# Retention plus phase-MLP kernel on one core: half of the fourth unit's output copy behind the fifth unit's masking, the sixth unit's scores ahead of the fifth's inner product

## The chip, the cores and the metric

One core of a Trainium2 chip runs the kernel. The metric is the device time of one execution in microseconds (us); lower is better. The kernel before was run three times: 164.02, 164.14 and 164.96 us, median 164.14 us.

Engine names below: PE multiplies matrices (PEld is its weight load), DVE is the vector engine, ACT the activation engine, POOL the general-purpose engine, SP the engine that only issues transfers. PE writes into PSUM banks; DVE and ACT read them from there.

## The reference: what is computed

Inputs are q, k and v of shape (4 batches, 8 heads, 768 positions, 64 columns) and four weight matrices. The first part is a recurrent retention per batch and head, the second a small phase network on its output:

```python
for t in range(S):
    state = gamma * state + outer(k[t], v[t])
    y[t] = scale * (q[t] @ state)
x = y with the heads side by side            # (4, 768, 512)
theta = x @ w_theta
zr, zi = x * cos(theta), x * sin(theta)
u = x + w_tok_r @ zr + w_tok_i @ zi          # mixes the 768 positions
out = u + maximum(u @ w_ch, 0)
```

## The kernel before: tiles, stages and what sets the order

The recurrence is computed in blocks. A *unit* is 256 positions of four heads of one batch, so there are 4 x 3 x 2 = 24 units, numbered from 0 in the code. Unit 3 is the fourth unit, unit 4 the fifth, unit 5 the sixth. Two successive units hold the same positions and the two halves of the heads. A unit passes through these steps:

- `ck`, `cq` or `cqs`, `cv`: k, q and v, as loaded, become bfloat16 (line 350 for v, tile `vb`).
- `Tk`, `Tq` (line 358): PE transposes k and q into one PSUM tile `kq_ps`; `E` copies it to `kqT` in SBUF, on ACT (line 138) or DVE (line 140).
- `A` (line 392): PE computes the *scores*, 16 small matmuls of `kqT` with itself, into the PSUM tile `at_ps`. There is one buffer of it. `m` (line 401, DVE) multiplies the scores by the causal mask into `at`.
- `I` (line 457): the *inner product* of q with the state carried from before (`sbd`), four matmuls; `Y` (line 469): the masked scores times v, 16 small matmuls added to the same PSUM tile; `ST` (line 419): the state's increment, 16 small matmuls into another part of that tile. The tile is `r_ps`, in two banks R0 and R1, one buffer each, so a unit's `I` waits until the unit before it has been read out of both.
- `S0`, `S1` (lines 437 and 441, DVE) add the increment to the state `s`; `SB` casts it into `sbd` for the next unit of the same heads, one half on each of two engines.
- `XB` (a copy, line 138 or 140) or `XA` (a multiplication, line 487): the *output copy*, which takes the unit's result from R0 (c = 0) and R1 (c = 1) into `xT`. This is in two halves, one for each bank.
- `Tx`, `Ex`: `xT` is transposed (line 501) and copied to `x_sb`; `Hh` (line 518) multiplies it with w_theta; `CN` (line 525, ACT) takes sine and cosine; `z` (line 532) multiplies. `Tw` and `Ew` (lines 540 and 140) transpose the token-mixing weights, `M` (line 563) sums over positions, `u`, `Tu`, `O`, `f` and `SO` form and store the output.

The order of all this is written out by hand: `ORDER` (lines 23 to 87) is a string of tokens, one for each step, and the kernel calls them in that order. A token's last letter names the engine (`v` DVE, `a` ACT, `p` POOL, `s` SP). No scheduler reorders: each engine executes its own instructions in the order in which the tokens issue them, and waits where an operand or a buffer is not ready. `XB.3.1.v` is thus the copy of half 1 of unit 3 on DVE, `m.4` the masking of unit 4, `E.5.v` the copy of unit 5's transposed k and q on DVE, `A.5` unit 5's scores, and `I.4` unit 4's inner product.

Of the kernel before, what the change touches and what calls it, by code (L numbers as in the profile page):

```python
# [28 lines left out]
Z.11 cqs.3.p Tq.3 Lv.3.s Tx.0 Tk.3 Z.3 ck.4.p Lv.4.s Lk.5.s Lq.5.s Lv.5.s Lq.6.s Lk.6.s Lv.6.s Lq.7.s E.3.a  # L29
SB.2.0.v I.2 Y.2 XB.2.1.a Ex.0.a cv.3.v cq.4.p Tk.4 Lq.8.s A.3 ST.3 Lk.7.s S0.3.v SB.3.0.a S1.3 Lv.7.s  # L30
Lk.8.s Tx.1 Tq.4 SB.3.1.p cv.4.p m.3 Pw.1.0 XB.2.0.a Ex.1.a I.3 Lv.8.s E.4.a cq.5.a Y.3 Pw.0.0 ST.4 Hh.0
ck.5.a S0.4.v XB.3.0.v XB.3.1.v cv.5.v CN.0.1 A.4 CN.0.0 Tq.5 Hh.1 Tk.5 SB.4.0.p SB.4.1.a Pw.0.1 Hh.2 m.4
E.5.v I.4 Y.4 ST.5 ck.6.a Tk.6 Tx.2 cq.6.a CN.1.1 CN.1.0 XA.4.1 A.5 XA.4.0 m.5 Lq.9.s Ex.2.v S0.5.v z.0.p
Tq.6 E.6.a CN.2.0 cv.6.p Hh.3 SB.5.0.v Tx.3 Tw.1.0 z.1.v SB.5.1.a Ew.1.0.v Ex.3.a CN.2.1 A.6 I.5 Y.5 ST.6
XA.5.0 z.2.v Tw.0.0 CN.3.0 Tx.4 CN.3.1 Ew.0.0.v S0.6.v XA.5.1 Ex.4.v Hh.4 CN.4.0 CN.4.1 Tw.0.1 M.0.1 Pw.1.1
z.3.v M.0.0 Tw.0.2 Pw.1.2 Ew.0.2.a SB.6.1.a Hh.5 z.4.p SB.6.0.p Lk.9.a M.0.3 ck.7.p cqs.7.p M.0.2 CN.5.1
# [770 lines left out]
```

## Time and profile before

| | before |
|---|---|
| runs, us | 164.02, 164.14, 164.96 |
| the profiled execution, us | 164.45 |
| its span, us | 162.7 |
| PE busy, us | 152.1 |
| DVE busy, us | 128.4 |
| ACT busy, us | 82.8 |
| POOL busy, us | 80.7 |
| granted clock of PE, share of full speed | 0.996 |

The span runs from the first to the last instruction of the profiled execution; the 1.7 us between it and that execution's time lie around the kernel. All positions in time below are us from the span's start. In a row of the timeline, several instructions of the same kind that follow each other are one row with their count, and an instruction's duration includes a part that overlaps the next one, so the distance between two starts is shorter than the duration. A remark in brackets says how long the engine had been idle before the row, and who ended that wait.

### The profile page before, as it was taken

The numbers are of one execution on the slowest core, as the hardware profiler recorded it, in microseconds if no ns is written. First come the engines' busy times: TensorE is split into PE (matmuls) and PEld (weight loads), VectorE is DVE, ScalarE is ACT, GpSimd is POOL, SyncE is SP. The second block draws the span as 40 slices with busy tenths as digits, with TensorE's granted clock in tenths as the row PEclk, the third lists the DMA queues.
The fourth block names the chain that finished last, engine by engine and source line by source line (L and its number), as shares of the span: only waits on it lengthen the run. The fifth ranks groups of instructions, "written<-read, shape, count | busy, mean of one in ns | idle before, by whom it ended". The sixth has DMA issues, their size and how long they took to land.

```text
span 162.7 us, 5046 instructions
## 1 busy us (share of the span) xinstructions
PE 152.1 (93%) x2043; PEld 90.8 (56%) x2072; DVE 128.4 (79%) x254; ACT 82.8 (51%) x151; POOL 80.7 (50%) x115
## 2 busy tenths in 40 slices
PE   5997979999999999999999999999999999999991
PEld 1354656656666555754454656544555446788650
DVE  5489687977993896994879796967988898796782
ACT  4967698994658336664443526761755506100010
POOL 7788089169206732550227499966468601540000
PEclk9999999999999999999999999999999999999998
DMA  4999999999999998969999998899999416533845
GB/s 123 319 309 236 298 318 244 265 229 216 202 208 195 308 236 190 276 153 266 317 318 204 124 296 137 214 185 266 233 275 142 82 28 181 160 118 102 225 170 219
DMA packets 62919, 34.93 MB, mean 215 GB/s; under 512 B 26416, under 2 KB 59952, under 8 KB 62896
## 3 DMA queue, kind: packets, MB, share of 16 engines
q1 hardware_dynamic: 51680, 23.73, 66.0%
q10 hardware_dynamic: 8528, 7.47, 15.4%
q0 software_dynamic: 2688, 3.41, 12.4%
q8 instruction: 16, 0.26, 0.7%
q14 instruction: 7, 0.06, 0.1%
HBM read 25.69 MB, written 6.29 MB: 197 GB/s over the span
## 4 chain that ended last, share of the span: by engine, by line
PE 85%; DVE 4%; ACT 4%; issue 2%; DMA 2%; POOL 0%; DVEq 0%; SPq 0%; POOLq 0%
PE y_ps L563 27%; PE th_ps L518 12%; PE o_ps L593 12%; PE zz L313 5%; PE r_ps L469 4%; PE kq_ps L358 4%; PE xw L681 3%; PE at_ps L392 3%; PE xwv L681 3%; PE w_ps L540 3%; PE r_ps L457 3%; PE vv L681 3%; PE x_ps L501 2%; DMA out_dram<-ot 2%; PE r_ps L419 2%
## 5 line engine op out<-in xcount | busy, mean ns | idle before, releaser
L563 PE MATMUL y_ps<-z,wti 128*128 128x512 bf16 x105 | 39.8, 379 | 1.2 <-issue 1.1
L563 PE MATMUL y_ps<-z,wtr 128*128 128x512 bf16 x100 | 37.9, 379 | 0.1
L401 DVE TENSOR_TENSOR at<-at_ps,mask 128x1024 bf16<-128x1024 f32 x24 | 29.2, 1217 | 0.1
L350 POOL TENSOR_TENSOR vb<-vf,vsc 128x512 bf16<-128x512 f32 x18 | 18.8, 1046 | 20.2 <-DMA vf<-in_v_dram 13.3
L518 PE MATMUL th_ps<-wth,xT 128*128 128x512 bf16 x88 | 24.2, 379 | 0.6
L593 PE MATMUL o_ps<-wch,uT 128*128 128x512 bf16 x85 | 22.2, 379 | 0.6 <-DMA out_dram<-ot 0.2
L525 ACT ACTIVATE cs<-th_ps,halfpi 128x512 bf16<-128x512 f32 x24 | 16.5, 686 | 10.1 <-DVE z L532 4.0
L532 POOL TENSOR_TENSOR z<-cs,x_sb 128x1024 bf16<-128x1024 bf16 x8 | 17.0, 2124 | 8.5 <-DVE z L532 4.7
L525 ACT ACTIVATE cs<-th_ps,zerob 128x512 bf16<-128x512 f32 x24 | 16.4, 685 | 8.2 <-PE th_ps L518 8.1
L138 ACT COPY kqT<-kq_ps 128x1024 bf16<-128x1024 bf16 x12 | 12.1, 1012 | 11.9 <-PE kq_ps L358 11.9
L140 POOL CAST sbd<-s 64x256 bf16<-64x256 f32 (+1 forms) x17 | 8.9, 525 | 18.3 <-DVE s L437 16.8
L599 DVE SCALAR_TENSOR_TENSOR ot<-o_ps,u 128x512 f32<-128x512 f32 x23 | 15.6, 687 | 2.7 <-PE o_ps L593 2.7
L570 DVE TENSOR_TENSOR u<-y_ps,x_sb 128x512 bf16<-128x512 f32 x18 | 12.4, 687 | 6.3 <-PE y_ps L563 6.1
L563 PEld LDWEIGHTS <-wtr 128*128 128x128 bf16 x108 | 10.5, 97 | 9.7
L563 PEld LDWEIGHTS <-wti 128*128 128x128 bf16 x108 | 10.5, 98 | 8.8 <-DVE wti L140 0.2
L518 PEld LDWEIGHTS <-xT 128*128 128x128 bf16 x96 | 8.8, 98 | 8.3
L138 ACT CAST sbd<-s 64x256 bf16<-64x256 f32 (+1 forms) x24 | 8.9, 372 | 7.8 <-DVE s L437 6.0
L593 PEld LDWEIGHTS <-uT 128*128 128x128 bf16 x92 | 8.3, 98 | 7.8 <-DMA uT<-u 0.2
L313 PE MATMUL zz<-zero 128*128 128x512 bf16 x27 | 10.1, 511 | 2.0 <-DVE part L233 1.9
L358 PE MATMUL kq_ps<-ident,kqb 128*128 128x128 bf16 x120 | 11.2, 220 | 0.8 <-ACT kqb L138 0.7
L138 ACT CAST kqb<-kqf 128x512 bf16<-128x512 f32 x17 | 10.3, 620 | 2.4 <-DMA kqf<-in_k_dram 2.3
L138 ACT CAST xT<-r_ps 128x256 bf16<-128x256 f32 x19 | 6.7, 371 | 9.3 <-PE r_ps L419 8.4
(127 smaller groups left out, 281.7 us busy)
## 6 DMA issues: line engine op xcount, KB each, us to landing
vf<-in_v_dram SPq DMA_DIRECT2D x20, 256.0 KB, 5.4
kqf<-in_k_dram SPq DMA_DIRECT2D x19, 256.0 KB, 4.6
kqf<-in_q_dram SPq DMA_DIRECT2D x17, 256.0 KB, 4.5
out_dram<-ot ACTq DMA_DIRECT2D x12, 256.0 KB, 3.1
out_dram<-ot SPq DMA_DIRECT2D x11, 256.0 KB, 2.8
kqf<-in_q_dram ACTq DMA_DIRECT2D x7, 256.0 KB, 5.0
kqf<-in_k_dram ACTq DMA_DIRECT2D x5, 256.0 KB, 5.5
vf<-in_v_dram ACTq DMA_DIRECT2D x4, 256.0 KB, 4.7
```

The source lines that it names most:

```text
L138: nc.scalar.copy(dst, src)
L313: nc.tensor.matmul(t, K["zero"][:, :P], K["zero"], start=True, stop=True)
L350: engines[e].tensor_mul(in_blocks(vb), by_token(raw["vf", n]), _bcast_last(K["vsc"][:, i, :, h * HU:(h + 1) * HU], D))
L358: nc.tensor.transpose(st["kq_ps", n][:, 4 * w + x, :], st["kqb", n][:, w, x * P:(x + 1) * P], K["ident"])
L401: nc.vector.tensor_mul(at.rearrange("p g j a t -> p (g j) (a t)"), st["at_ps", n].rearrange("p g j a t -> p (g j) (a t)"), _bcast_mid(K["m ...
L518: nc.tensor.matmul(th_ps, st["xT", C][:, j, :], K["wth"][:, j, :], start=(j == 0), stop=(j == 3))
L525: nc.scalar.activation(st["cs", C][:, w, :], st["th_ps", C], AF.Sin, bias=K["zerob" if w else "halfpi"], scale=1.0)
L532: engines[e].tensor_mul(st["z", b][:, c], st["cs", C], _bcast_mid(x_of(C), 2))
L563: nc.tensor.matmul(st["y", t], K["wT"][r][:, s0, t0 * P:(t0 + 1) * P], st["z", b][:, s0, r, :], start=(done == 0 and r == 0), stop=(done = ...
L593: nc.tensor.matmul(o_ps, st["uT", t][:, j, :], K["wch"][:, j, :], start=(j == 0), stop=(j == nD - 1))
L599: nc.vector.scalar_tensor_tensor(st["ot", t], st["o", t], 0.0, st["u", t], ALU.max, ALU.add)
L681: nc.tensor.matmul(o, a, m_, start=(phase == 0 and n == 0 and k != 1), stop=n == nT - 1, skip_group_check=True)
```

## The change

Two tokens change places in the string:

```diff
-ck.5.a S0.4.v XB.3.0.v XB.3.1.v cv.5.v CN.0.1 A.4 CN.0.0 Tq.5 Hh.1 Tk.5 SB.4.0.p SB.4.1.a Pw.0.1 Hh.2 m.4
-E.5.v I.4 Y.4 ST.5 ck.6.a Tk.6 Tx.2 cq.6.a CN.1.1 CN.1.0 XA.4.1 A.5 XA.4.0 m.5 Lq.9.s Ex.2.v S0.5.v z.0.p
+ck.5.a S0.4.v XB.3.0.v cv.5.v CN.0.1 A.4 CN.0.0 Tq.5 Hh.1 Tk.5 SB.4.0.p SB.4.1.a Pw.0.1 Hh.2 m.4 XB.3.1.v
+E.5.v A.5 I.4 Y.4 ST.5 ck.6.a Tk.6 Tx.2 cq.6.a CN.1.1 CN.1.0 XA.4.1 XA.4.0 m.5 Lq.9.s Ex.2.v S0.5.v z.0.p
```

On DVE, one copy moves past two instructions. These are DVE's rows from unit 4's state update on; the first `L140 CAST xT<-r_ps` is `XB.3.0`, the second `XB.3.1`, `L350` is `cv.5`, `L401` is `m.4`, `L140 COPY kqT` is `E.5`, and `L487` is unit 4's output copy.

```order
 L437 TENSOR_TENSOR s_444<-r_ps,s_444 128x128
-L140 CAST xT<-r_ps 128x256 x2
-L350 TENSOR_TENSOR vb<-vf,vsc 128x512
-L401 TENSOR_TENSOR at<-at_ps,mask 128x1024
+L140 CAST xT<-r_ps 128x256
+L350 TENSOR_TENSOR vb<-vf,vsc 128x512
+L401 TENSOR_TENSOR at<-at_ps,mask 128x1024
+L140 CAST xT<-r_ps 128x256
 L140 COPY kqT<-kq_ps 128x1024
 L487 TENSOR_TENSOR xT<-r_ps,qx 128x256 x2
```

The second copy now stands between `m.4` and `E.5`. The rows that follow are in the same order as before: `m.5` stays behind unit 4's two output multiplications.

On PE, the 16 matmuls and 16 weight loads of `A.5` move up. This is PE before, where the last matmuls of `Hh.2` (line 518) are followed by `I.4` (line 457):

```order
L518 MATMUL th_ps<-wth,xT 128x512
L518 LDWEIGHTS xT
L518 MATMUL th_ps<-wth,xT 128x512
L457 LDWEIGHTS sbd_96 [waits Activation_49,Pool_49]
L457 MATMUL r_ps<-kqT,sbd_96 128x128 [waits PE_49]
```

And this is the same place now, with `A.5` (line 392) behind `Hh.2`:

```order
L518 MATMUL th_ps<-wth,xT 128x512
L518 LDWEIGHTS xT
L518 MATMUL th_ps<-wth,xT 128x512
L392 LDWEIGHTS kqT [waits DVE_49]
L392 MATMUL at_ps<-kqT 64x128 [waits PE_49]
```

`I.4` comes behind `A.5`, then `Y.4`, `ST.5`, `Tk.6` and `Tx.2` as before, and then `Tq.6` directly, where `A.5` used to stand between `Tx.2` and `Tq.6`. The first weight load of `A.5` now holds a wait on DVE, for `E.5`. Nothing changes on ACT, POOL and SP, and no instruction is added or removed.

## The prediction

> **What bounds the kernel now.** I read the page first, then busy time by stage, then the timeline of PE, DVE and ACT around the change.
>
> ```profile
> span 162.7 us, 5046 instructions
> PE 152.1 (93%) x2043; PEld 90.8 (56%) x2072; DVE 128.4 (79%) x254; ACT 82.8 (51%) x151; POOL 80.7 (50%) x115
> PE 85%; DVE 4%; ACT 4%; issue 2%; DMA 2%; POOL 0%; DVEq 0%; SPq 0%; POOLq 0%
> ```
>
> The third row is the chain of work that ended last, by engine: PE holds 85% of it. By stage (columns: the stretch, its length, busy us of PE, PEld, DVE, ACT and POOL, the granted clock, the DMA share, GB/s):
>
> ```profile
> 20.00:24.00 4.00, 3.05 (x67) 1.98 (x66) 3.20 (x8) 3.94 (x8) 3.55 (x6) 1.00 1.14 315
> 24.00:28.00 4.00, 3.95 (x78) 2.64 (x77) 2.94 (x5) 3.40 (x7) 3.49 (x3) 1.00 1.16 256
> 28.00:32.00 4.00, 3.70 (x76) 2.50 (x77) 3.75 (x9) 3.93 (x7) 1.11 (x2) 1.00 1.15 262
> 40.00:60.00 20.00, 19.42 (x322) 12.33 (x326) 16.30 (x33) 11.49 (x20) 8.52 (x9) 1.00 1.18 236
> ```
>
> PE stands idle for about 1 us at 20 to 24, before the change takes hold; from 24 on it works 3.95 of 4, 3.70 of 4, 19.42 of 20. So whatever PE loses at the place of the change has little idle time behind it to be made up in, and whatever it could gain is bounded by the idle time that stands there now. PE at this place, unit by unit (start, duration, line, what, count):
>
> ```profile
> 22.08 1.04 PE L518 MATMUL th_ps<-wth,xT 128*128 128x512 bf16 x3
> 23.05 0.42 PE L392 MATMUL at_ps<-kqT 64*64 64x128 bf16 x16
> 24.50 0.39 PE L358 MATMUL kq_ps<-ident,kqb 128*128 128x128 bf16 x4
> 24.73 1.03 PE L518 MATMUL th_ps<-wth,xT 128*128 128x512 bf16 x4
> 25.59 0.40 PE L457 MATMUL r_ps<-kqT,sbd 128*128 128x128 bf16 x4
> 25.91 0.42 PE L469 MATMUL r_ps<-at,vb 64*64 64x128 bf16 x16
> 26.16 0.29 PE L419 MATMUL r_ps<-vb,kqb 64*64 64x64 bf16 x16
> 26.39 0.40 PE L358 MATMUL kq_ps<-ident,kqb 128*128 128x128 bf16 x4
> 26.62 0.39 PE L501 MATMUL x_ps<-ident,xT 128*128 128x128 bf16 x4
> 26.94 0.42 PE L392 MATMUL at_ps<-kqT 64*64 64x128 bf16 x16
> 27.29 0.40 PE L358 MATMUL kq_ps<-ident,kqb 128*128 128x128 bf16 x4
> 28.79 0.38 PE L501 MATMUL x_ps<-ident,xT 128*128 128x128 bf16 x4 [0.24 <-ACT kqT L138]
> 29.45 0.42 PE L392 MATMUL at_ps<-kqT 64*64 64x128 bf16 x16
> 29.81 0.41 PE L457 MATMUL r_ps<-kqT,sbd 128*128 128x128 bf16 x4
> 30.15 0.42 PE L469 MATMUL r_ps<-at,vb 64*64 64x128 bf16 x16
> ```
>
> These are A.4 at 23.05, Tk.5 at 24.50, Hh.2 at 24.73, I.4 at 25.59, Y.4, ST.5, Tk.6, Tx.2, A.5 at 26.94, Tq.6 at 27.29, Tx.3 at 28.79, and A.6, I.5, Y.5. Neither I.4 nor A.5 nor Y.4 waited: the only wait is 0.24 before Tx.3, for the copy E.6 on ACT. DVE in the same stretch:
>
> ```profile
> 22.23 0.29 DVE L437 TENSOR_TENSOR s<-r_ps,s 128x128 f32<-128x128 f32 x1 [0.67 <-PE r_ps L419]
> 22.43 0.75 DVE L140 CAST xT<-r_ps 128x256 bf16<-128x256 f32 x2
> 23.10 0.68 DVE L350 TENSOR_TENSOR vb<-vf,vsc 128x512 bf16<-128x512 f32 x1
> 23.69 1.22 DVE L401 TENSOR_TENSOR at<-at_ps,mask 128x1024 bf16<-128x1024 f32 x1
> 24.93 0.69 DVE L140 COPY kqT<-kq_ps 128x1024 bf16<-128x1024 bf16 x1
> 26.55 0.76 DVE L487 TENSOR_TENSOR xT<-r_ps,qx 128x256 bf16<-128x256 f32 x2 [0.93 <-PE r_ps L419]
> 27.42 1.23 DVE L401 TENSOR_TENSOR at<-at_ps,mask 128x1024 bf16<-128x1024 f32 x1
> 28.56 0.42 DVE L140 COPY x_sb<-x_ps 128x512 bf16<-128x512 bf16 x1
> 28.89 0.28 DVE L437 TENSOR_TENSOR s<-r_ps,s 128x128 f32<-128x128 f32 x1
> 30.02 0.54 DVE L140 COPY wti<-w_ps 128x768 bf16<-128x768 bf16 x1
> 30.77 0.42 DVE L487 TENSOR_TENSOR xT<-r_ps,qx 128x256 bf16<-128x256 f32 x1 [0.21 <-PE r_ps L419]
> ```
>
> S0.4, then XB.3.0 and XB.3.1 (one row, x2), cv.5, m.4, E.5, an idle 0.93, XA.4.1 and XA.4.0, m.5 at 27.42, Ex.2, S0.5, Ew.1.0, XA.5.0.
>
> **The copy XB.3.1, moved behind m.4.** The pair and its follower lie 23.10 - 22.43 = 0.67 apart, so one copy holds DVE for 0.335. Without it cv.5 starts at 22.77 and leaves DVE free at 22.77 + 0.59 (its distance to m.4) = 23.36. But m.4 also needs A.4, which ends at 23.05 + 0.42 = 23.47; m.5 started 0.06 after A.5 ended (26.94 + 0.42 = 27.36, then 27.42), so m.4 starts at 23.53, 0.16 earlier than now. Nobody waits for it sooner: Y.4, its reader, did not wait. XB.3.1 follows at 23.53 + 1.14 (the distance of m.5 to Ex.2) = 24.67 and ends at about 25.09, before I.4 needs the bank R1 that it empties. E.5 starts at 24.67 + 0.335 = 25.00. Tk.5 has ended by 24.50 + 0.39 = 24.89, so DVE itself is what E.5 waits for, and it is 0.07 late: ends 25.69 instead of 25.62. The readers of XB.3.1's own result, Hh.3 and Tx.3, come after 27.5.
>
> **A.5, moved ahead of I.4.** Its first weight load now needs E.5. What such a hand-off takes is shown by unit 0:
>
> ```profile
> 8.57 0.69 DVE L140 COPY kqT<-kq_ps 128x1024 bf16<-128x1024 bf16 x1 [1.35 <-PE kq_ps L358]
> 9.31 0.42 PE L392 MATMUL at_ps<-kqT 64*64 64x128 bf16 x16
> ```
>
> The copy ended at 9.26 and the scores started at 9.31, 0.05 later. A.5 therefore starts at 25.69 + 0.05 = 25.74. With E.5 in time it would start about 0.97 behind Hh.2 (as A.4 behind Hh.0, 22.08 to 23.05), at 25.70; the wait itself is worth about 0.04, and it is Hh.2 that hides the rest of E.5. Without that cover the price would be the whole 0.69 of the copy. As to the cost of going from large to small matmuls: Hh.2 to I.4 is 0.86, Hh.0 to A.4 is 0.97, so 0.11 goes with the switch to 64*64. [...]
>
> Behind A.5, by distances between starts: I.4 0.36 later (29.45 to 29.81) at 26.10; Y.4 0.34 later (29.81 to 30.15) at 26.44; ST.5 0.25 later at 26.69; Tk.6 0.23 later at 26.92; Tx.2 0.23 later at 27.15; Tq.6 0.23 later (as Tx.2 behind Tk.6) at 27.38. Before, Tq.6 started at 27.29. PE's own loss up to here is 0.09.
>
> **What follows from it.** ACT in this stretch:
>
> ```profile
> 27.73 1.01 ACT L138 COPY kqT<-kq_ps 128x1024 bf16<-128x1024 bf16 x1 [0.55 <-PE kq_ps L358]
> 28.64 0.69 ACT L525 ACTIVATE cs<-th_ps,halfpi 128x512 bf16<-128x512 f32 x1
> 29.36 0.40 ACT L138 CAST sbd<-s 64x256 bf16<-64x256 f32 x1
> ```
>
> E.6 waited 0.55 for Tq.6, so it moves with Tq.6 by 0.09, and so do Tx.3, which waits for E.6, and A.6. The larger delay is on DVE. ST.5 moved from 26.16 to 26.69, by 0.53, because A.5 now stands ahead of it; XA.4.1, which waited for ST.5, moves to 27.08. m.5 cannot use the scores being ready at 26.16, since it stands behind XA.4 in DVE's order: it starts 0.67 after XA.4.1, at 27.75, which is 0.33 later than now (the other 0.2 was spent waiting for A.5, or lay between XA.4 and m.5). Ex.2 follows at 28.89, S0.5 at 28.89 + 0.33 = 29.22, ending 29.50. Its reader on ACT, half of SB.5, started at 29.36 because ACT was busy until 28.64 + 0.69 = 29.33; S0.5 had ended at 29.17. Now ACT is free at 29.42 and S0.5 is done at 29.50: with the 0.05 of a hand-off it starts at 29.55, 0.19 later, and ends at 29.95. I.5 needs it. PE is ready for I.5 at 29.81 + 0.09 = 29.90; 0.05 after the cast is 30.00. So I.5 and all behind it on PE are 0.19 late. Y.5 at 30.34 finds m.5 finished (27.75 + 1.23 = 28.98). XA.5.0 waited for ST.6 with 0.21 of idle DVE; it moves by 0.19 to 30.96, while DVE, 0.33 late, finishes Ew.1.0 at 30.35 + 0.54 = 30.89 and does not add to that.
>
> Sum: 0.04 for the wait at A.5, 0.05 for the rearranged switches, 0.10 for the state cast that now ends last: 0.19 us, carried to the end by a PE that has hardly any idle time left. Against the profiled execution, 164.45 + 0.19 = 164.64; that execution was 0.31 above the median of the runs, so against the median 164.14 + 0.19 = 164.3 us.
>
> **Bounds of the unknown terms.** No row shows A.5 directly behind Hh.2, or I.4 behind A.5 here. From below: if A.5 took I.4's slot at 25.59, Tq.6 would start at 27.23, a gain of 0.06. From above: the whole 0.53 by which ST.5 moves passes on to PE. I take 0.19, near the middle, because the two waits for E.5 and for the state cast are both read from rows beside them.
>
> **The rivals.**
>
> *No loss at all* (164.1): E.5's 0.07 disappears under Hh.2 and the 0.33 of DVE under the casts, as ACT's own occupancy hid S0.5 by 0.16 until now. For it: every single term is below 0.1. Against it: the terms all have the same sign.
>
> *The whole delay reaches PE* (164.14 + 0.53 = 164.7): it happens if DVE's lateness meets a PE that waits for DVE's weight copies between 30 and 36. Against it, DVE has idle time in this row:
>
> ```profile
> 36.21 1.02 DVE L140 COPY wti<-w_ps 128x768 bf16<-128x768 bf16 x2 [0.88 <-PE w_ps L540]
> ```
>
> *Somewhat faster* (163.8): the moved order makes the 0.24 wait before Tx.3 disappear and A.5 takes I.4's slot: 0.24 + 0.06 = 0.30. For it: it is the only idle time that PE has here. Against it: Tx.3 waits for E.6 and E.6 for Tq.6, which gets no earlier than by that 0.06.
>
> *Slower by over 1%* (165.8): the lateness of the masking accumulates. Each of the units 5 to 9 has the same loop, ST to XA to m to S0 to SB to I; if PE waited in each for its state cast by the 0.33 that m.5 is late, five units would give 1.65. It decides from the point where unit 6's cast, too, ends later than PE is ready for I.6. Against it: the waits don't add when the same lateness is met again, and the 0.88 of idle DVE at 36.21 ends it.
>
> *Faster by over 1%*: this would need 1.64, and from 24 on no row at this place has PE waiting for more than 0.24.
>
> **How the numbers follow.** The forecast (late by 0.1 to 0.35) has a chance of 0.55, no loss 0.23, the whole delay 0.10, somewhat faster 0.07, slower by over 1% 0.03, faster by over 1% 0.02. About 1% is what a measurement of this kernel can tell from no change: its three runs span 0.6%. The range takes the bounds of the sum, 164.08 and 164.67, widened on either side by the 0.31 by which one execution stood off the median: 163.7 to 165.0. Within 1%, that is 162.5 to 165.8, lie all cases but the last two: 0.95.
>
> **What would show it.** In the changed kernel's timeline the scores of unit 5 should follow Hh.2 at about 25.74, with a short wait for kqT of DVE; XB.3.1 alone at about 24.67 and E.5 at 25.00; Tq.6 near 27.38; XA.4.1 near 27.08 after more than the present 0.93 of idle DVE; m.5 near 27.75 without a wait; the state cast on ACT near 29.55 and I.5 near 30.00. The prediction is wrong if Tq.6 starts before 27.29, if I.5 starts as early as before, or if PE has new waits of more than 0.1 later than 32.

## The result, and the profile after

The changed kernel takes 165.26 us in the median (164.35 to 166.5, 22 executions); the kernel before, run beside it, 164.21 us (22 executions, from 164.02). The ratio is 1.0053, with an interval of 1.0034 to 1.0073; it leaves out one slow execution of the kernel before (169.25) and is not the ratio of the two medians, which are 1.05 us apart. This is within 1%, as forecast, but it is 0.9 to 1.05 us slower and lies outside the predicted range of 163.7 to 165.0.

The profiled execution of the changed kernel took 164.6 us, one of its shorter ones, so it shows only a part of that loss. From its page (span, busy time, chain that ended last):

```profile
span 162.9 us, 5045 instructions
PE 150.8 (93%) x2043; PEld 90.6 (56%) x2072; DVE 129.5 (80%) x254; ACT 82.9 (51%) x151; POOL 80.5 (49%) x115
PE 77%; DVE 10%; POOL 4%; issue 3%; DMA 2%; ACT 1%; DVEq 0%; POOLq 0%
```

The same work but for one instruction that only waits (5045 against 5046; the experiments come back to it), and still PE's kernel. This execution had come through the start 0.26 us sooner than the profiled one of before (A.4 starts at 22.79 instead of 23.05), so 0.26 is added, here and in the section on the prediction, to each time of it around the change that is compared with before or with the prediction. PE at the place of the change, in the timeline (start, duration, line, what, count):

```profile
22.79 0.42 PE L392 MATMUL at_ps<-kqT 64*64 64x128 bf16 x16
...
24.46 1.03 PE L518 MATMUL th_ps<-wth,xT 128*128 128x512 bf16 x4
25.55 0.42 PE L392 MATMUL at_ps<-kqT 64*64 64x128 bf16 x16
25.90 0.41 PE L457 MATMUL r_ps<-kqT,sbd 128*128 128x128 bf16 x4
...
26.48 0.29 PE L419 MATMUL r_ps<-vb,kqb 64*64 64x64 bf16 x16
...
27.16 0.39 PE L358 MATMUL kq_ps<-ident,kqb 128*128 128x128 bf16 x4
...
28.65 0.38 PE L501 MATMUL x_ps<-ident,xT 128*128 128x128 bf16 x4 [0.24 <-ACT kqT L138]
29.13 0.49 PE L540 MATMUL w_ps<-ident,row 128*128 128x128 bf16 x6
29.56 0.42 PE L392 MATMUL at_ps<-kqT 64*64 64x128 bf16 x16
29.91 0.41 PE L457 MATMUL r_ps<-kqT,sbd 128*128 128x128 bf16 x4
```

A.5 stands behind Hh.2, and down to Tx.3 everything is within 0.1 us of what was forecast. Then comes a wait that the prediction does not have: Tw.1.0 (line 540) starts 0.48 behind Tx.3, where it was 0.24 before (28.79 to 29.03). Its row in the kernel before:

```profile
29.03 0.50 PE L540 MATMUL w_ps<-ident,row 128*128 128x128 bf16 x6
```

DVE in the same stretch of the changed kernel shows whom it waits for:

```profile
22.17 0.41 DVE L140 CAST xT<-r_ps 128x256 bf16<-128x256 f32 x1
22.50 0.93 DVE L350 TENSOR_TENSOR vb<-vf,vsc 128x512 bf16<-128x512 f32 x1
23.35 1.21 DVE L401 TENSOR_TENSOR at<-at_ps,mask 128x1024 bf16<-128x1024 f32 x1
24.48 0.41 DVE L140 CAST xT<-r_ps 128x256 bf16<-128x256 f32 x1
24.82 0.68 DVE L140 COPY kqT<-kq_ps 128x1024 bf16<-128x1024 bf16 x1
26.86 0.76 DVE L487 TENSOR_TENSOR xT<-r_ps,qx 128x256 bf16<-128x256 f32 x2 [1.37 <-PE r_ps L419]
27.53 1.22 DVE L401 TENSOR_TENSOR at<-at_ps,mask 128x1024 bf16<-128x1024 f32 x1
28.67 0.41 DVE L140 COPY x_sb<-x_ps 128x512 bf16<-128x512 bf16 x1
```

Ex.2 (28.67) ends at 29.08, and Tw.1.0 starts at 29.13. In the code, the transposed k and q, the transposed `xT` and the transposed weights share the two buffers of tag `tr`. Tx.3 takes the one that E.6 empties, Tw.1.0 the one that Ex.2 empties, and Ex.2 stands behind m.5, which is late.

On the whole span I compare the starts of PE's weight loads with those of before's profiled execution, each execution set to zero at 20 us. The changed kernel is 0.36 late at 30, 0.26 late from 38 on, and still 0.26 late at 125. So the place of the change costs 0.26 us in this execution. With the start that was 0.26 sooner, PE stands at 125 us where it stood before; the 0.15 by which this execution took longer comes behind 153 us (the last output matmuls, line 759, start at 158.14 instead of 157.99). The rest of the median's 1.05 us is not in this execution; it had to be looked for in others.

### The profile page after: what moved, and what is told of

It is laid out like the page before. It is cut to its first block, busy times and chain, and to the rows that moved or that the text cites. A ratio compares the mean times of both kernels' runs of the same rounds, so it can differ in the third digit from the quotient of the medians.

```text
span 162.9 us, 5045 instructions
## 1 busy us (share of the span) xinstructions
PE 150.8 (93%) x2043; PEld 90.6 (56%) x2072; DVE 129.5 (80%) x254; ACT 82.9 (51%) x151; POOL 80.5 (49%) x115
## 4 chain that ended last, share of the span: by engine, by line
PE 77%; DVE 10%; POOL 4%; issue 3%; DMA 2%; ACT 1%; DVEq 0%; POOLq 0%
PE y_ps L563 28%; PE th_ps L518 10%; PE o_ps L593 10%; PE r_ps L469 5%; DVE at L401 4%; PE at_ps L392 4%; PE r_ps L457 3%; PE xwv L681 3%; PE w_ps L540 3%; PE kq_ps L358 3%; DMA uT<-u 2%; PE xw L681 2%; PE r_ps L419 2%; PE vv L681 2%; PE x_ps L501 1%
## 5 line engine op out<-in xcount | busy, mean ns | idle before, releaser
L401 DVE TENSOR_TENSOR at<-at_ps,mask 128x1024 bf16<-128x1024 f32 x24 | 29.2, 1216 | 0.5 <-PE at_ps L392 0.5
L350 POOL TENSOR_TENSOR vb<-vf,vsc 128x512 bf16<-128x512 f32 x18 | 18.7, 1041 | 21.8 <-DMA vf<-in_v_dram 21.2
L140 POOL CAST sbd<-s 64x256 bf16<-64x256 f32 (+1 forms) x17 | 8.8, 520 | 17.1 <-DVE s L437 15.7
L532 DVE TENSOR_TENSOR z<-cs,x_sb 128x1024 bf16<-128x1024 bf16 x16 | 10.9, 684 | 0.8 <-DMA x_sb<-xT 0.6
```

The costliest lines, as they stand in the source:

```text
L350: engines[e].tensor_mul(in_blocks(vb), by_token(raw["vf", n]), _bcast_last(K["vsc"][:, i, :, h * HU:(h + 1) * HU], D))
L401: nc.vector.tensor_mul(at.rearrange("p g j a t -> p (g j) (a t)"), st["at_ps", n].rearrange("p g j a t -> p (g j) (a t)"), _bcast_mid(K["m ...
L532: engines[e].tensor_mul(st["z", b][:, c], st["cs", C], _bcast_mid(x_of(C), 2))
```

## The experiments

The table puts the two kernels and fifteen runs together; the sections below say what each run was for. Columns: median, and ratio to the kernel before with its interval; the share of executions more than 0.6 us above the kernel's own fastest, called late ones below (wherever their granted clock is on record it was 0.996 to 1.0, except for two of the run with less warm-up, 0.99, and one of "after, k.23 early", 0.989, so it isn't the clock); then, in the profiled execution, PE's delay at 38 to 70 us and at 125 us (as above), the wait of POOL's cqs.20 at about 106.5, and the wait of DVE's z.18 at about 118.

| kernel | median, us | ratio | late ones | PE at 38-70 | PE at 125 | cqs.20 waits | z.18 waits |
|---|---|---|---|---|---|---|---|
| before (all) | 164.21 to 164.51 | 1 | 41 of 149 | 0 | 0 | - | - |
| after | 165.26 | 1.0053 [1.0034, 1.0073] | 14 of 22 | 0.26 | 0.26 | 0.35 | 0.17 |
| copy alone | 164.47 | 1.0011 [0.9988, 1.0034] | 3 of 12 | -0.02 | 0.39 | - | 1.05 |
| scores alone | 165.34 | 1.0054 [1.0032, 1.0076] | 9 of 12 | 0.13 | 0.12 | 0.21 | - |
| after, again | 165.25 | 1.0044 [1.0024, 1.0064] | 7 of 12 | 0.26 | 0.87 | 0.31 | 0.81 |
| after, Ex.2 ahead of m.5 | 165.08 | 1.0039 [1.0012, 1.0066] | 8 of 12 | 0.27 | 0.98 | 0.24 | 0.97 |
| after, one more on DVE | 164.82 | 1.0033 [1.0007, 1.0059] | 4 of 12 | 0.26 | 0.34 | - | - |
| before, one fewer on DVE | 165.29 | 1.0049 [1.0025, 1.0074] | 8 of 12 | 0.19 | 1.63 | 0.64 | 1.27 |
| before, one more on DVE | 164.86 | 1.0015 [0.9988, 1.0042] | 7 of 12 | -0.09 | 0.64 | 0.79 | 0.60 |
| before, PE delayed, less warm-up | 166.11 | 1.0099 [1.007, 1.0129] | 5 of 6 | 0.86 | 0.91 | - | - |
| before, PE delayed | 164.69 | 1.0025 [0.9998, 1.0053] | 5 of 12 | 0.13 | 0.13 | - | 0.18 |
| after, q.20 early | 165.14 | 1.0039 [1.002, 1.0059] | 0 of 11 | 0.26 | 0.89 | - | - |
| before, q.20 early | 165.01 | 1.0036 [1.0017, 1.0055] | 3 of 12 | -0.09 | 0.53 | - | - |
| after, q.20 for a store | 164.55 | 1.0025 [0.9996, 1.0054] | 5 of 12 | 0.26 | 0.25 | - | - |
| before, q.20 for a store | 164.40 | 1.0009 [0.9976, 1.0041] | 3 of 12 | -0.08 | -0.03 | - | - |
| after, k.23 early | 164.92 | 1.0026 [1.0009, 1.0043] | 3 of 12 | 0.26 | 0.52 | 0.26 | - |
| before, k.23 early | 164.28 | 0.9993 [0.9973, 1.0012] | 2 of 12 | 0.13 | 0.26 | - | - |

Two things limit what the table can say. The kernel before was run beside each group of runs, and its share of late executions was not the same each time: 5 of 22, 7 of 35, 8 of 29, 15 of 34 and 6 of 29. And the delays are counted from 20 us on, while executions differ ahead of that too: the row of PE that starts at 20.76 in the kernel before (line 457) starts between 20.45 and 21.31 in the profiled executions with all warm-up matmuls.

### The two halves, each alone, and the change again

Only the copy's token moved:

```diff
-ck.5.a S0.4.v XB.3.0.v XB.3.1.v cv.5.v ... Hh.2 m.4
+ck.5.a S0.4.v XB.3.0.v cv.5.v ... Hh.2 m.4 XB.3.1.v
```

> Only the fourth unit's second output copy goes behind the fifth unit's masking; the sixth unit's scores stay where they were. Theory 1 (the scores' place costs the time, through the state increment that comes 0.5 us later): no loss, E.5 about 0.07 us late with nobody waiting, ratio to before 0.998 to 1.002. Rival 2 (the copy's place costs it, because the fifth unit's masking and the copy of kqT stand in another order against the landing v): most of the loss is here, ratio 1.004 or more. Rival 3 (any change of the early order disturbs the loads): ratio above 1.003 here too, with runs spread over 1 us or more.

Only the scores' token moved:

```diff
-E.5.v I.4 Y.4 ST.5 ... XA.4.1 A.5 XA.4.0 m.5
+E.5.v A.5 I.4 Y.4 ST.5 ... XA.4.1 XA.4.0 m.5
```

> Only the sixth unit's scores go ahead of the fifth unit's inner product; the copy stays. Theory 1: the whole loss, ratio about 1.005; the first weight transpose (Tw.1.0) waits about 0.2 us for DVE's copy Ex.2, as in the changed kernel. Rival 2: ratio below 1.002.

And both, as in the change:

> The changed kernel once more, for a second profile and more times. Both theories: ratio 1.003 to 1.007. If the loss beyond the 0.37 us seen in the first profile comes from arrivals of loads that the order before absorbed, a profile of a longer run shows PE waiting for a transfer, or for a copy behind one, later than 24 us.

The copy alone costs nothing that can be measured; the scores alone cost as much as the whole change. In the scores-alone run A.5 starts at 25.41, behind E.5 and 0.07 ahead of the end of Hh.2's last record (24.45 + 1.03 = 25.48); so what A.5 waits for is E.5, as forecast, and not that end. In PE's delay the two are not independent: -0.02 for the copy, 0.13 for the scores, 0.26 for both. The copy makes E.5 later (24.82 with it, 24.65 with the scores alone, A.4 at 22.79 and 22.77), and only with the scores moved does PE wait for E.5.

The repeat is where a part of the missing time became visible. Its profiled execution took 165.39 us, 0.8 more than the first one. Up to 110 us both are alike; then DVE's z.18 (line 532) and PE's I.21 (line 457) read so in the repeat, the first row from DVE's timeline, the second from PE's:

```profile
119.02 0.69 DVE L532 TENSOR_TENSOR z<-cs,x_sb 128x1024 bf16<-128x1024 bf16 x1 [0.81 <-DMA x_sb<-xT]
...
122.32 0.39 PE L457 MATMUL r_ps<-kqT,sbd 128*128 128x128 bf16 x4 [0.46 <-DVE xT L140]
```

In the kernel before the same two rows have no wait:

```profile
117.60 0.69 DVE L532 TENSOR_TENSOR z<-cs,x_sb 128x1024 bf16<-128x1024 bf16 x1
...
121.42 0.40 PE L457 MATMUL r_ps<-kqT,sbd 128*128 128x128 bf16 x4
```

z.18 needs `x_sb` of tile 18, which the transposing transfer Dx.18 brings; when that is late, all of DVE behind it is late (S0.21, m.21, S1.21, the copy XB.20.0), and I.21 waits for the bank that XB.20.0 empties. In the five profiles where z.18 waits by 0.6 or more this costs 0.4 to 1.2 us, 90 us behind the edit. The copy alone has it too in its profiled execution, so it isn't made by the change. Late executions are there in the kernel before as well, only fewer: 41 of 149, against 14 of 22 and 7 of 12 after.

That every late execution comes from this wait is not shown. Five profiled executions are late ones (leaving out the run with less warm-up). Four of them have the wait (the repeat, Ex.2 first, one fewer and one more in the kernel before); the fifth, of the kernel before with q.20 early, has none, and is instead the one that reaches line 457 last, at 21.31. No late execution of the kernel before itself was profiled.

### Ex.2 ahead of m.5

The wait of Tw.1.0 for Ex.2 should go when Ex.2 stands first:

```diff
-XA.4.1 XA.4.0 m.5 Lq.9.s Ex.2.v S0.5.v
+XA.4.1 XA.4.0 Ex.2.v m.5 Lq.9.s S0.5.v
```

> The changed kernel with DVE's copy Ex.2 ahead of the sixth unit's masking m.5. Ex.2 then ends near 27.9 instead of 29.1, Tx.3 takes its bank and Tw.1.0 that of E.6. Theory 1: the waits of 0.24 us before Tx.3 and before Tw.1.0 go, the state cast on ACT (29.71) becomes the last, I.5 starts near 29.76 instead of 29.91, and the time falls by 0.15 us or a little more against the changed kernel, ratio to before about 1.004. If the waits on the two banks are the whole cause, the ratio falls to 1.001 or less. Rival 2: no change against the changed kernel.

The wait of Tw.1.0 went (it starts 0.22 behind Tx.3), but the profiled execution has another in its place, 0.44 of Hh.3 for ACT's `cs`, and PE is as late as in the change (0.27). That wait appears in an execution of the kernel before with one instruction fewer too (0.38), where nothing moved at this place, so it may have come from ACT's loads and not from the edit. The run doesn't settle what the wait for Ex.2 alone is worth.

### One instruction in DVE's stream

What sets apart the four profiles with the scores moved that were seen so far is a row at 101 us. (PE's rows near 100 us stand at the same times in the two first profiles, since the sooner start and the 0.26 of the change cancel; from here on times are compared as they stand.) The answer for line 140 between 101 and 103 us, in the kernel before (DVEq EVENT_SEMAPHORE is a separate instruction of DVE that only waits, 21 ns in these rows):

```profile
L140 DVEq EVENT_SEMAPHORE  x1: 21/21/21, 101.4 to 101.4; - x1
L140 DVE COPY s<-r_ps x1: 292/292/292, 101.8 to 101.8; 128x128 f32<-128x128 f32 x1
```

The wait for unit 18's increment is over at 101.4, and the copy S0.18 starts 0.4 later. The profile puts its idle time down to PE's A.18 (line 392), which S0.18 does not read and whose record ends at 101.52 (101.12 + 0.40); nothing that S0.18 needs is seen to come at 101.8. In the changed kernel:

```profile
L140 DVEq EVENT_SEMAPHORE  x1: 21/21/21, 101.4 to 101.4; - x1
L140 DVE COPY s<-r_ps x1: 292/292/292, 101.4 to 101.4; 128x128 f32<-128x128 f32 x1
```

There S0.18 follows at once, and the two instructions XA.17 behind it start 0.41 after it (101.44 to 101.85) instead of 0.21. Counted from the start of DVE's stream, it is in both kernels the same place, the 192nd of the instructions in the trace, that is held up. The stream had become one shorter. The answers for line 401, the masking, before and after:

```profile
L401 DVEq EVENT_SEMAPHORE  x3: 21/21/21, 9.8 to 83.2; - x3
```

```profile
L401 DVEq EVENT_SEMAPHORE  x2: 21/21/21, 9.6 to 83.2; - x2
```

m.5 used to wait for A.5 on PE and for earlier work of DVE; one of these two waits stood in an instruction of its own. With A.5 ahead of ST.5, the wait of XA.4 for ST.5 covers A.5, and the separate wait is gone (5046 instructions on the page before, 5045 after). So the sentence ahead of the prediction that nothing is removed holds for the instructions that work, not for DVE's stream. Three kernels test whether this is what makes the late executions. The changed kernel with a memset of one column ahead of S0.4, where DVE is idle:

```diff
-S0.4.v XB.3.0.v cv.5.v
+J.v S0.4.v XB.3.0.v cv.5.v
```

> The changed kernel with one more, tiny instruction on DVE (a memset of one column that nobody reads), put ahead of S0.4, where DVE stands idle. The changed kernel needs one instruction fewer on DVE than the kernel before, since m.5 no longer needs a separate wait for PE; from m.5 on every later DVE instruction stands one place earlier in DVE's stream, and a stall of about 0.4 us that sits at one place of that stream (at 101.4 in the kernel before, in front of the copy S0.18) falls on the instruction behind it. With the extra instruction the places are again those of the kernel before. Theory A (the median's rise is the local loss of 0.26 us plus what this shift does to the transfers after 101 us): about 164.5, ratio near 1.0015, the copy S0.18 again 0.4 behind its wait and the cqs.20 on POOL without a wait. Theory B (every delay of 0.26 us early on is amplified later by the transfers): as the changed kernel, about 165.2, ratio near 1.005. Theory C (the extra loss is neither): anything else.

The kernel before with one instruction fewer among the constants:

```diff
-nc.vector.tensor_scalar_mul(par2, par, -2.0)
-nc.vector.tensor_scalar_add(posq, posq, par2)
+nc.vector.tensor_scalar(out=posq, in0=posq, scalar1=par, scalar2=par,
+                        op0=ALU.subtract, op1=ALU.subtract)
```

> The kernel before with one tiny instruction fewer on DVE among the constants (two operations on a 128x12 tile written as one), so that DVE's stream is one place shorter from the start and its places after m.5 are those of the changed kernel; nothing else moves, and the scores stand where they stood. Theory A (the shift does the late part of the loss): about 164.9 to 165.0, ratio near 1.004, with XA.17 about 0.15 earlier against PE, the load of q for unit 20 landing about 0.3 later and cqs.20 waiting for it. Theory B (a delay early on is amplified) and Theory C: no change, 164.25, ratio within 1.000 plus or minus 0.002.

The kernel before with the memset:

> The kernel before with the same tiny extra DVE instruction ahead of S0.4, so that DVE's stream is one place longer than before from there on. The stall at that place of the stream then falls on the wait in front of S0.18, where DVE stands idle anyway. Theory A in its strict form (what counts is how early XA.17 and the transpose behind it start against the loads): S0.18 and XA.17 0.2 to 0.35 earlier than in the kernel before, and a loss of 0.3 to 0.8 us as in the run with one fewer. If the extra instruction costs nothing (164.25), only the place of the shorter stream matters, or the shift doesn't matter at all. Theories B and C: 164.25, ratio within 1.000 plus or minus 0.002.

With one instruction fewer on DVE and the scores where they were, the kernel before is as slow as the change: 165.29 us, 8 of 12 late, and the ratio's interval lies clear of 1. Its profile has all the marks of the changed one: S0.18 right behind its wait, XA.17 0.41 behind S0.18, and the waits of cqs.20 and z.18:

```profile
101.80 0.29 DVE L140 COPY s<-r_ps 128x128 f32<-128x128 f32 x1 [1.20 <-PE r_ps L419]
107.62 1.04 POOL L344 TENSOR_TENSOR kqb<-kqf,qsc 128x512 bf16<-128x512 f32 x1 [0.64 <-PE r_ps L469]
119.94 0.69 DVE L532 TENSOR_TENSOR z<-cs,x_sb 128x1024 bf16<-128x1024 bf16 x1 [1.27 <-DMA x_sb<-xT]
```

With one more in the changed kernel, 4 of 12 are late and the median falls to 164.82, less far than the expected 164.5; its interval overlaps that of the change, so this run alone does not show a gain. One more in the kernel before gives 7 of 12 late ones too, as the strict form of its expectation had it, though its ratio can't be told from 1. Taken together, the kernels with the hold-up in front of S0.18 and nothing else at work (before, copy alone, one more in the changed kernel, PE delayed) have 53 late executions of 185 (12 of 36 without the kernel before); those with it elsewhere (after, twice, scores alone, Ex.2 first, one fewer, one more in the kernel before) have 53 of 82.

### A delay of PE alone

A rival has it that any early delay of this size would make the transfers collide. PE is held up by doing the four transposes of Tx.2 twice:

```diff
-for j in range(4):
+for j in 2 * list(range(4)) if C == 2 else range(4):
```

The first run also left out two pairs of the warm-up matmuls (`Z.29 Z.2`), to keep PE's stream at its old length.

> The kernel before with the four transposes of Tx.2 done twice into the same tile: a pure delay of PE of about 0.23 us at 26.8, with DVE's stream as it was. Two pairs of the warm-up matmuls at the very start are left out, so that PE's stream has its old places again behind Tx.2. Theory A: only the delay itself, about 164.45, ratio near 1.0014. Theory B (any early delay of this size is amplified): about 165.1, ratio near 1.005.

This run does not isolate the delay. PE at the start, in this kernel:

```profile
1.93 4.45 PE L313 MATMUL zz<-zero 128*128 128x512 bf16 x10 [1.93 <-DVE part L233]
7.76 1.04 PE L358 MATMUL kq_ps<-ident,kqb 128*128 128x128 bf16 x8 [1.38 <-POOL kqb L140]
```

In the kernel before the eight transposes took 0.65 (7.88 to 8.53) behind 14 warm-up matmuls; here 1.04 behind 10; they had started 0.12 sooner (7.76 against 7.88), and PE was 0.74 late by 20 us (line 457 at 21.50 instead of 20.76). A wait of 0.54 for `vb` at 41.86 adds to it, so the 166.11 says nothing on the rival. From start to start the eight take 0.97 here (7.76 to 8.73), 0.12 each, and 0.58 in the kernel before (7.88 to 8.46); the four of Tk.6 there take 0.23 (26.39 to 26.62), 0.06 each, which is twice the pace. What slows them is not shown: in the changed kernel too PE stood idle ahead of them (1.19, here 1.38), behind 14 warm-up matmuls in 4.62 (here 10 in 4.45), and there they took 0.62. The run again, with all warm-up matmuls:

> The kernel before with the transposes of Tx.2 done twice and all warm-up matmuls kept (in the first run of this kind leaving out two pairs of them cost about 0.75 us at the start, since PE's first transposes ran at half the pace, and hid the answer). Theory A: the 0.22 of the four transposes less what the wait of 0.24 before Tx.3 takes up, 0.1 to 0.2 in all: median 164.35 to 164.6, with as few slow executions as the kernel before. Theory B (any early delay makes the late transfers collide): 165 or more, with two thirds slow.

Here the 0.22 of the transposes is seen at 29 us, 0.13 of it remains from 38 on, and it stays 0.13 to the end; 5 of 12 are late, the median is 164.69, and the ratio can't be told from 1. The rival's 165 us did not come, though the interval reaches up to 1.0053 and 5 of 12 lies between a quarter and two thirds; so the rival is made unlikely, not excluded.

### The load of q for unit 20

How does a hold-up at 101 us reach a transfer at 118? The rows between, in the kernel before (DVE, SP's queue, POOL):

```profile
102.01 0.75 DVE L487 TENSOR_TENSOR xT<-r_ps,qx 128x256 bf16<-128x256 f32 x2
...
102.78 1.19 SPq L508 DMA_TRANSPOSE x_sb<-xT  x1
...
106.52 1.04 POOL L344 TENSOR_TENSOR kqb<-kqf,qsc 128x512 bf16<-128x512 f32 x1
```

and in the changed one:

```profile
101.85 0.76 DVE L487 TENSOR_TENSOR xT<-r_ps,qx 128x256 bf16<-128x256 f32 x2
...
102.63 1.29 SPq L508 DMA_TRANSPOSE x_sb<-xT  x1
...
106.90 1.04 POOL L344 TENSOR_TENSOR kqb<-kqf,qsc 128x512 bf16<-128x512 f32 x1 [0.35 <-PE o_ps L593]
```

XA.17 and the transposing transfer Dx.16 start 0.15 sooner. The loads of q for units 20 and 22, issued by ACT at 101.49 in both, land 5.3 us after their issue instead of 5.0 (the answer for line 160). cqs.20 on POOL, which needs the first, waits (the profile names PE, whose work had long been done), and with it the transposes Dk.20 that SP issues are late, 107.97 instead of 107.59, and so are the next issues in SP's queue, down to the load of k for unit 23. Dx.18 itself is not issued later. The last two, and z.18, in the kernel before (its z.18 at 117.60 without a wait is shown above):

```profile
111.74 0.57 SPq L164 DMA_DIRECT2D kqf<-in_k_dram  x1
...
113.75 1.19 SPq L508 DMA_TRANSPOSE x_sb<-xT  x1
```

and in the changed one:

```profile
112.06 0.57 SPq L164 DMA_DIRECT2D kqf<-in_k_dram  x1
...
113.74 1.19 SPq L508 DMA_TRANSPOSE x_sb<-xT  x1
...
118.10 0.69 DVE L532 TENSOR_TENSOR z<-cs,x_sb 128x1024 bf16<-128x1024 bf16 x1 [0.17 <-DMA x_sb<-xT]
```

Dx.18 lands 3.8 us after its issue in the kernel before, about 4.3 in the changed one (when z.18 starts) and 4.9 in the repeat. It is the transfer that takes longer, behind a load that was issued 0.3 later; in the copy-alone run it takes 4.7 although that load was not issued later, so this is not the only way.

All seven profiles in which S0.18 follows its wait at once and this load of q stands at its old place have the wait of cqs.20, 0.21 to 0.79; none of the ten others has it. The step from there to z.18 is looser: five of the seven have a wait of z.18, and so have two of the ten (copy alone, 1.05, and PE delayed, 0.18).

To cut this chain, the load is issued 0.6 us sooner, ahead of a store and an activation on ACT:

```diff
-Lv.19.a SO.1.a CN.14.0 Dx.16 Lq.20.a f.10 Lq.22.a
+Lv.19.a Lq.20.a SO.1.a CN.14.0 Dx.16 f.10 Lq.22.a
```

> The changed kernel with the load of q for unit 20 issued on ACT's queue ahead of the store of tile 1 instead of behind it and behind one activation, about 0.6 us earlier. Nothing moves on PE, DVE, POOL and SP. Theory A says that the late part of the loss runs over this load: it lands too late in the changed kernel, so POOL's cqs.20 waits for it (0.35 in the profiled execution), so the transposes of unit 20 and all that SP issues behind them are late, and DVE's z.18 waits for its transpose Dx.18 in two of three executions. Then cqs.20 starts without a wait, the share of executions more than 0.6 us over the fastest falls from about two thirds to a quarter, and the median is near 164.55 (ratio 1.0018). Rival D (the late wait of z.18 comes from something else that is shifted with DVE's stream): median still near 165.2, ratio 1.005.

> The kernel before with the same load earlier. Theory A: the load is in time here already in most executions, so little changes: median 164.15 to 164.25, ratio 0.998 to 1.000, with at most the slow quarter of its executions becoming rarer. Rival D: 164.25, ratio 1.000. If it becomes slower, the earlier load costs something by itself, and the run on the changed kernel has to be read beside that.

In the changed kernel cqs.20 and z.18 no longer wait, and not one of 11 executions is late by its own measure: 165.01 to 165.59. But both kernels lose 0.62 at one place, shown by ACT's rows in the changed kernel with this load early:

```profile
100.99 0.61 ACTq L160 DMA_DIRECT2D kqf<-in_q_dram  x1
101.64 0.61 ACTq L604 DMA_DIRECT2D out_dram<-ot  x1
102.30 0.69 ACT L525 ACTIVATE cs<-th_ps,halfpi 128x512 bf16<-128x512 f32 x1 [1.06 <-issue]
```

The activation CN.14.0 stood at 101.47 before; it now waits while ACT issues two transfers, and PE waits for it (0.46 at 103.04). Without that cost the load and the store change places:

```diff
-Lv.19.a SO.1.a CN.14.0 Dx.16 Lq.20.a f.10 Lq.22.a
+Lv.19.a Lq.20.a CN.14.0 Dx.16 f.10 Lq.22.a SO.1.a
```

> The changed kernel with the load of q for unit 20 and the store of tile 1 exchanged on ACT's queue: the load is issued ahead of the activation CN.14.0 as in the run with the load earlier, and the store behind it, so that only 0.1 us more of issuing stands ahead of CN.14.0 instead of 0.6. In the run with the load earlier PE waited 0.46 more for CN.14.0 and lost 0.61 in every execution, which hid the answer. Theory A (the late part of the loss runs over this load): that fixed loss is gone, cqs.20 and z.18 don't wait, median 164.5 to 164.6 (ratio 1.0015 to 1.002), hardly an execution over 165.1. Rival D: 165.2.

> The kernel before with the same exchange. Theory A: its own slow quarter of executions comes over the same load and the same transpose, so they become rare: median 164.1 to 164.2 (ratio about 0.998), a candidate that beats both kernels. Rival D: 164.3 to 164.5 as the kernel before.

The changed kernel comes to 164.55 us, as expected: 0.34 over the kernel before, of which 0.26 is the place of the change. The interval (0.9996 to 1.0054) still takes in the ratios of the change itself, 1.0044 and 1.0053, so the gain is likely and not shown. S0.18 still follows at once there, and cqs.20 has no wait:

```profile
101.40 0.29 DVE L140 COPY s<-r_ps 128x128 f32<-128x128 f32 x1 [1.21 <-PE r_ps L419]
```

```profile
106.46 1.04 POOL L344 TENSOR_TENSOR kqb<-kqf,qsc 128x512 bf16<-128x512 f32 x1
```

Late executions did not become as rare as expected, 5 of 12, which can't be told from 21 of 34; with the load early by either edit they are 5 of 23 in the changed kernel, near the share of the kernel before, but 11 of these 23 are from the edit that delays every execution by 0.62. In the kernel before the exchange gained nothing (ratio 1.0009), so its own late quarter may come over something else; that is left open.

### The load of k for unit 23

The other end of the chain: Dx.18 stands in SP's queue behind a load of 256 KB, that of k for unit 23. It is issued ahead of Dk.20, where SP is idle for 1 us:

```diff
-Lk.22.s Dk.20 ... Dk.21 ... Y.19 Lk.23.s ST.20
+Lk.22.s Lk.23.s Dk.20 ... Dk.21 ... Y.19 ST.20
```

> The changed kernel with the load of k for unit 23 issued by SP ahead of the transposes Dk.20, where SP stands idle for about 1 us, instead of behind Dk.21, so that its 256 KB no longer go just ahead of Dx.18. Nothing moves on PE, DVE, POOL. If the wait of z.18 comes from Dx.18 standing behind this load in the transfers, the share of slow executions falls to a quarter or less and the median is near 164.55 (ratio 1.0018). If the wait comes from elsewhere (the instruction fetch at 115 to 116, or the lateness of Dk.20 itself): median still near 165.2. If the load now delays the transposes of unit 20: slower than the changed kernel.

> The kernel before with the same load of k for unit 23 earlier. If Dx.18 behind this load makes the slow quarter of its executions, they become rarer and the median falls to about 164.1 (ratio 0.998 to 0.999); otherwise 164.25; slower if the load now gets in the way of the transposes of unit 20.

In the changed kernel cqs.20 still waits (0.26), yet z.18 doesn't, and 3 of 12 are late: 164.92 us, although the edit costs 0.26 of its own at 113 us (PE's delay goes from 0.26 to 0.52; 0.13 in the kernel before). This fits a late cqs.20 doing harm only through what stands ahead of Dx.18; it is one profile and 12 executions. The kernel before gains nothing that can be measured (0.9993).

None of the versions is measurably faster than the kernel before.

## Why the prediction was mostly right in its steps and wrong in its sum

**The steps at the place of the change**, but for the last, came as forecast. With the 0.26 added: XB.3.1 at 24.74 (forecast 24.67), E.5 25.08 (25.00), A.5 25.81 (25.74), Tq.6 27.42 (27.38), XA.4.1 27.12 (27.08) after 1.37 of idle DVE, m.5 27.79 without a wait (27.75). The state cast of unit 5 on ACT:

```profile
29.31 0.40 ACT L138 CAST sbd<-s 64x256 bf16<-64x256 f32 x1
```

that is 29.57, forecast 29.55. The 0.09 of PE's own loss measured 0.13 (Tq.6 27.29 to 27.42).

**I.5 did not come at 30.00 but at 30.17.** The 0.10 for the state cast was the wrong term. The cast was as late as I said, but PE did not wait for it, since it had been held up ahead of A.6 already, by Tw.1.0's wait for Ex.2. I had moved Ex.2 by 0.33 in the working and used it only to place S0.5; who waits for the buffer that it empties I did not ask. PE is 0.36 late at 30 us instead of 0.19; 0.10 of that is taken up by 38 us, and 0.26 stay.

**E.5 was 0.08 later than I said** because of a duration that I took over. cv.5 (line 350) took 0.68 before and takes 0.93 here; with the scores alone moved it takes 0.68, with the copy alone 0.93, and in four more runs with the copy moved (the repeat, one more on DVE, q.20 early, q.20 for a store) 0.89 to 0.93. Its new place is beside a cast on POOL. POOL's timeline, before and after:

```profile
22.71 0.42 POOL L140 CAST sbd<-s 64x256 bf16<-64x256 f32 x1
```

```profile
22.45 0.42 POOL L140 CAST sbd<-s 64x256 bf16<-64x256 f32 x1
```

Before, cv.5 started at 23.10, 0.03 ahead of the cast's end at 23.13; now it starts at 22.50, 0.05 behind the cast's start, with 0.37 of the cast still to come (22.50 to 22.87), and takes 0.25 longer. Another such pair stands in the kernel before, DVE's row first and POOL's second:

```profile
91.09 0.68 DVE L350 TENSOR_TENSOR vb<-vf,vsc 128x512 bf16<-128x512 f32 x1
...
91.24 0.80 POOL L140 CAST sbd<-s 64x256 bf16<-64x256 f32 x1 [1.64 <-DVE s L437]
```

Here cv starts first and takes its 0.68, and the cast, 0.15 behind it, takes 0.80 instead of 0.42. In both pairs the one that starts second takes longer; why, is not shown. I had put cv.5 at 22.77 beside a cast of 22.71 to 23.13 and kept its old distance to m.4.

**The main error is the sentence that the loss is carried to the end by a PE that has hardly any idle time left.** It holds for the 0.26. But a quarter of the executions of the kernel before (41 of 149) are late, and with the change nearly two thirds are (21 of 34). The prediction says nothing of how: one wait instruction fewer on DVE, and, in four of the five late executions that were profiled, a transfer that lands late near 118 us. The step that failed here stands ahead of the sum: that no instruction is removed. DVE's stream is one shorter, and the shift by one place goes with most of the loss. My range took the spread of a single execution, 0.31, as noise that stays; with late executions in the majority, the median moves over to them. By the runs, 0.26 of the 1.05 are the place of the change (0.34 between the medians with the load of q exchanged for a store), and most of the rest goes with DVE's stream (0.97 in the kernel before with one instruction fewer, of which 0.19 is in PE's delay at 38 already). What is argued and not shown: what holds DVE up at that place, why a transposing transfer that starts 0.15 sooner goes with two loads that land 0.3 later, and that this is the way by which the shift makes late executions, since none of the edits that take out a part of it brings the median back clear of noise.

**The rivals.** No loss at all and somewhat faster are refuted. "The whole delay reaches PE" (164.7) was near for the wrong reason: 0.36 of the 0.53 got there, 0.13 of it PE's own and the rest by a wait of the weight transposes for a buffer at 29 us; that rival named a wait for the weight copies, at 30 to 36. Slower by over 1% did not come, and masking's lateness did not add up from unit to unit: after 38 us PE's delay is constant for 60 us. A new wait of PE later than 32, which I had named as a sign of being wrong, is there in the repeat (0.46 at 122.32).

## What to carry to other kernels

For each instruction that becomes late, ask not only who reads its result but who waits for the buffer that it frees; and for each that becomes early, what it will run beside (cv.5, 0.93 us beside POOL's cast instead of 0.68). When times of one kernel spread, look for the wait that makes the long executions before the edit is costed: an edit can change how often it happens without coming near it, and the median jumps when that passes a half. A moved instruction can also add or take away a separate wait instruction and so shift everything behind it in its engine's stream, which a control with one idle instruction more or fewer can show, given enough executions.

## What the runs showed of the hardware that I had not expected

- DVE starts the 192nd instruction of its stream in the trace late. In the kernel before that is S0.18, 0.40 behind the wait in front of it (101.40 to 101.80); in the changed one it is the next, XA.17, 0.41 behind the start of S0.18 (101.44 to 101.85) instead of 0.21. In the kernel before with one more instruction the 192nd is the wait itself, and S0.18 (101.31) and XA.17 (101.52) both follow at once. The rows at 101 to 103 us of the other runs fit this count: S0.18 stands behind 1.57 or 1.58 of idle DVE where the stream has the length of before, and behind 1.20 or 1.21 where it is one shorter. Why it is this place is not shown.
- ACT starts an instruction late at the same count. Its 191st is a wait that ends at 128.46 in the kernel before, and the 192nd (line 525) starts at 128.81, 0.36 later; in the changed kernel it is 0.35 (128.45 to 128.80). Of the 18 other instructions that stand right behind such a wait in the kernel before, 11 start 0.03 to 0.05 behind it.
- The profile's table of queues lists 16 packets of "instruction" kind on queue 8 (0.26 MB) and 7 on queue 14 (0.06 MB) during the execution, in both kernels; one of queue 8 goes from 115.11 to 116.01 in the kernel before. One of queue 14 starts at 103.71 in the kernel before and at 103.34 in the changed one, 1.9 and 1.5 us behind the late starts at 101.80 and 101.85, so these starts did not wait for it; whether the two have to do with each other is not shown.
- In the changed kernel with the load of q early, ACT spends 0.61 us each on issuing a load and a store at 101 us, and the activation behind them starts at 102.30 instead of 101.47.
- With four warm-up matmuls fewer PE's first eight transposes took 1.04 instead of 0.65, and this execution was 0.74 late by 20 us; the latest of the profiled executions with all warm-up matmuls was 0.55 late there.
